# Windowed attention and a softplus feed-forward on one core: due times for the first 368 operations from a table, zero key columns by VectorE, the last block stored in smaller pieces

## The chip, the core and the metric

The kernel runs on one core of a Trainium2 chip. A core has five engines that work through queues of their own, in order: TensorE (PE in the profile; PEld is its weight load), VectorE (DVE), ScalarE (ACT), GpSimd (POOL) and SyncE (SP), which here only issues DMAs. ScalarE can issue DMAs too. The engines wait for each other and for DMAs by semaphores. The metric is the device time of one execution in microseconds (us).

## The reference

Attention with a causal window of 64 over 8 sequences of 576 positions, 8 heads of 64, and then a feed-forward layer with a softplus between its two products. All inputs and outputs are float32.

```python
scores = scale * np.matmul(q, k.transpose(0, 1, 3, 2))     # q, k, v: (8, 8, 576, 64)
mask = (rel >= 0) & (rel < window)                         # rel = query - key, window = 64
attn = softmax(np.where(mask, scores, -1e9))
x = np.matmul(attn, v)                                     # heads side by side: (4608, 512)
h = x @ w_in                                               # w_in: (512, 2048)
g = np.maximum(h, 0.0) + np.log1p(np.exp(-np.abs(h)))
out = g @ w_out                                            # w_out: (2048, 512)
```

## The kernel before

The 4608 rows are cut into 12 blocks `g` of 384 rows (three column tiles `j` of 128). The feed-forward's inner width is cut into 16 blocks `f` of 128. For every block of rows there are four head pairs `hp` of attention and then 16 steps of feed-forward. The first two blocks of rows work interleaved: block 0 with weight blocks 0 to 7, block 1 with all 16, block 0 with the rest (its partial sums wait in DRAM meanwhile), and then blocks 2 to 11 one after another.

All products are made in float32 accuracy from several passes: every operand is split into a rounded part and a remainder. The weights arrive as 64-bit words of 1 MB a block and are converted on the chip before they can be used.

The operations have these names, and the numbers behind them are the block and the head pair, or the block and the weight block:

- conversion of a weight block `f`: `load` (SP's DMA), `abs` (ScalarE, line 297), `c2`, `c3`, `c4` (VectorE, lines 298, 300, 302), `hi` (ScalarE, line 304), `lo` (VectorE, line 305)
- attention of a head pair: `q`, `k` (loads), `S` (PE, the scores, line 367 in the first three blocks, 411 later), `R` (VectorE, mask and row minima, line 338), `E` (ScalarE, exponentials, line 436), `sum` and `N` (VectorE, reciprocals and normalisation, lines 444 to 451), `T` and `cp` (in the first two blocks PE transposes, line 487, and ScalarE copies, line 490; later a DMA transposes), `V` (PE, the product with v, lines 498 and 590), `x0` and `x1` (the split of the result, ScalarE and VectorE, lines 504, 505)
- feed-forward step: `U` (PE, 12 matmuls of 384 columns, line 622), `soft` (ScalarE, three functions, lines 626 to 628), `m` (VectorE, line 634), `g0` (ScalarE in the first two blocks, line 636), `g1` (VectorE, line 637), `D` (PE, 9 matmuls of 512 columns into three banks, one for each `j`, line 646). `U` of a step writes one of two banks and waits until `m` of two steps before has read it.

No engine's queue is written by hand. Every operation is recorded with its engine, a planned cost, its dependencies and the buffers that it opens and uses, and a planner (`arrange`) lists them in time: of the operations that could start on an engine it takes the one with the earliest due time. The due times come from the function `dues` at first, and then eight rounds of `arrange` forward and `latest` backward follow, which give every operation the latest start that still meets the end. The round with the earliest planned end sets the order in which the instructions are issued. Constants of the planner are the delays `RESULT`, the DMA rate `BYTES_PER_US`, the delay `LAUNCH` and the first free time of each engine.

In the first block of rows there are no keys ahead of row 0. `load_k` lets GpSimd set the first 64 key columns to zero there (line 354), in four buffers, and loads the rest. GpSimd comes to it behind the masks and the zeros of `setup`.

The last step of a block copies the three banks of sums to SBUF (line 681) and stores them (line 684): tiles 0 and 1 in one DMA of 512 KB, tile 2 in one of 256 KB, both from SP.

Of the kernel before, what the change touches and what calls it, by code (L numbers as in the profile page):

```python
# [8 lines left out]
F32 = mybir.dt.float32  # L9
# [26 lines left out]

RESULT = {"PE": 0.25, "DVE": 0.12, "ACT": 0.15, "POOL": 0.2, "SP": 2.0}
BYTES_PER_US = 390e3
LAUNCH = 1.3

# [29 lines left out]
def arrange(ops, rings):  # L70

    for r in rings.values():
        r.taken = list(r.held)
    free = {"PE": 0.0, "DVE": 5.0, "ACT": 2.1, "POOL": 0.8, "SP": 0.8}
    pipe = 2.2
    left = {id(o): len(o.deps) for o in ops}
# [6 lines left out]
    while len(order) < len(ops):  # L83
        best = None
        for e, waiting in open_ops.items():
# [20 lines left out]
            t = max(free[e], min(at for at, _ in could))  # L106
            o = min((o for at, o in could if at <= t + 1e-9), key=lambda o: o.due)
            if best is None or t < best[0]:
# [7 lines left out]
        if o.nbytes:  # L116
            pipe = max(pipe, t + o.cost + LAUNCH) + o.nbytes / BYTES_PER_US
            o.end = pipe + RESULT["SP"]
        for b in o.opens:
# [55 lines left out]
def window_attention_softplus_ffn(  # L175
# [83 lines left out]
    def setup():  # L259
        nc.scalar.preload_act_table_set("natural_log_exp_and_others")  # L260
        nc.gpsimd.memset(wide, 0.0)
        for sign, op, base in ((1, ALU.is_gt, 0), (-1, ALU.is_ge, CH)):
            nc.gpsimd.affine_select(
                out=wide, in_=wide, pattern=[[sign, W]], compare_op=op, fill=FAR, base=base, channel_multiplier=-sign
            )
        nc.vector.memset(v_two[0][0:CH, 0, :], 0.0)
        for i in (1, 0, 2):
            nc.vector.tensor_copy(mask_q[0:CH, i, :], wide[0:CH, 0:P])
            nc.vector.tensor_copy(mask_q[CH:P, i, :], wide[CH:P, CH:W])
            if i:  # L270
                half = heads[i - 1]
                nc.vector.memset(mask_q[half, i, 0:CH], FAR)
# [12 lines left out]
    def convert(f):  # L285
# [28 lines left out]
    def attention(g, hp):  # L314
# [27 lines left out]
        if quad:  # L342
# [9 lines left out]
            def load_k():  # L352
                if skip:
                    nc.gpsimd.memset(qk(1)[:, 0:CH], 0.0)
# [26 lines left out]
        else:  # L381
# [22 lines left out]
            for j in range(NJ):  # L404
# [153 lines left out]
        for hh in range(2):  # L558
# [50 lines left out]
    sums_of, part, spilled = {}, {}, []  # L609
    ups, downs, stores = [], [], []  # L610

    def ffn(n, g, f, first, last):
# [12 lines left out]
        def soft():  # L625
# [24 lines left out]

        d = add("PE", 2.06, down, deps=[h, lo, *downs[-1:]], opens=acc if first else [], uses=[*gt, w_all[f]] + ([] if first else acc), name=f"D{g}.{f}")
# [141 lines left out]
```

## Time and profile before

| | us |
|---|---|
| median of 3 runs | 963.73 |
| lowest and highest of them | 963.46, 964.05 |
| the profiled execution | 965.21 |
| its span in the trace | 963.4 |
| mean granted clock of TensorE in it | 0.993 |

The profile shows one execution. Times are from the start of its span. A row of the timeline has the start, the length, the engine, the line and the operation with its tiles; where the engine was idle before it, the idle time and what ended it stand behind in brackets. Rows of equal instructions are merged (x24). Lines are those of the kernel before.

### The profile page before, as it was taken

How to read it: one execution, taken by the hardware profiler on the slowest of the kernel's cores; microseconds unless marked ns; L12 is line 12 of the kernel's file. 1: busy time of each engine (PE TensorE's matmuls, PEld its weight loads, DVE VectorE, ACT ScalarE, POOL GpSimd, SP SyncE). 2: the span in 40 equal slices, each digit the busy share in tenths (PEclk: the TensorE clock that was granted, in tenths of full speed). 3: DMA queues.
4: the chain of work that ended last, by engine and by line, in shares of the span. 5: the costliest groups of instructions: out<-in, count | busy, mean ns of one | idle time of the engine just before them, and what ended most of it. 6: DMA issues, size and time to landing. Idle time of an engine off the chain costs nothing.

```text
span 963.4 us, 16889 instructions
## 1 busy us (share of the span) xinstructions
PE 939.7 (98%) x6128; PEld 848.6 (88%) x6128; DVE 784.6 (81%) x1760; ACT 740.5 (77%) x1685; POOL 4.5 (0%) x18
## 2 busy tenths in 40 slices
PE   5899999999999999999999999999999999999997
PEld 4678888999999999998999999999999999998996
DVE  7999977898798888889879889879888887975333
ACT  6899877888788788778878778778878887875443
POOL 1000000000000000000000000000000000000000
PEclk7999999999999999999999999999999999999999
DMA  9961225575347345344445535535635464521000
GB/s 364 422 231 44 61 71 121 131 178 124 90 129 138 98 139 116 94 117 128 122 99 145 137 76 145 132 89 140 127 86 150 116 111 99 148 52 34 34 1 33
DMA packets 196516, 117.37 MB, mean 122 GB/s; under 512 B 130192, under 2 KB 187536, under 8 KB 194384
## 3 DMA queue, kind: packets, MB, share of 16 engines
q1 hardware_dynamic: 196144, 115.90, 46.0%
q8 instruction: 48, 0.79, 0.4%
q10 hardware_dynamic: 288, 0.39, 0.1%
q14 instruction: 36, 0.29, 0.1%
HBM read 74.58 MB, written 10.22 MB: 88 GB/s over the span
## 4 chain that ended last, share of the span: by engine, by line
PE 91%; DVE 6%; ACT 1%; issue 1%; POOL 0%; POOLq 0%; ACTq 0%
PE ps_o L646 40%; PE ps_h L622 40%; PE ps_a L590 6%; PE ps_a L411 5%; DVE work L300 1%; DVE work L302 1%; DVE w L305 1%; ACT st L436 1%; DVE st L338 1%; DVE work L298 1%; DVE u L634 0%; DVE g L637 0%; PE ps_a L367 0%; DVE st L451 0%; DVE x L505 0%
## 5 line engine op out<-in xcount | busy, mean ns | idle before, releaser
L622 PE MATMUL ps_h<-x,w 128*128 128x384 f32 x2304 | 435.2, 338 | 4.2 <-DVE u L634 3.2
L646 PE MATMUL ps_o<-w,g 128*128 128x512 f32 x1728 | 424.9, 394 | 0.0
L622 PEld LDWEIGHTS ps_h<-x,w 128*128 128x128 f32 x2304 | 401.9, 188 | 15.0 <-DVE u L634 3.9
L646 PEld LDWEIGHTS ps_o<-w,g 128*128 128x128 f32 x1728 | 320.3, 188 | 60.4 <-ACT u L626 0.2
L626 ACT ACTIVATE u<-ps_h 128x384 f32<-128x384 f32 x192 | 93.8, 488 | 138.2 <-PE ps_h L622 134.9
L634 DVE SCALAR_TENSOR_TENSOR u<-ps_h,u 128x384 f32<-128x384 f32 x192 | 106.3, 554 | 95.8 <-ACT u L628 93.5
L436 ACT ACTIVATE st<-st,mn 128x128 f32<-128x128 f32 x288 | 111.7, 389 | 24.2 <-DVE st L428 19.1
L637 DVE TENSOR_TENSOR g<-u,g 128x384 fp32r<-128x384 f32 x192 | 106.3, 554 | 10.1 <-ACT g L636 5.8
L628 ACT ACTIVATE u<-u 128x384 f32<-128x384 f32 x192 | 100.9, 525 | 6.1
L627 ACT ACTIVATE u<-u 128x384 f32<-128x384 f32 x192 | 100.8, 525 | 6.1
L338 DVE CUSTOM_DVE_ANT_0 st<-ps_a,wide 128x192 f32<-128x192 f32 x176 | 53.3, 351 | 13.8 <-PE ps_a L411 13.8
L636 ACT CAST g<-u 128x384 fp32r<-128x384 f32 x112 | 56.5, 505 | 9.8 <-DVE u L634 9.0
L590 PEld LDWEIGHTS <-v 128*128 128x128 bf16 x1136 | 54.5, 98 | 9.6 <-issue 7.2
L590 PE MATMUL ps_a<-tr,v 128*128 128x128 bf16 (+1 forms) x1136 | 60.3, 211 | 0.0
L411 PEld LDWEIGHTS ps_a<-k,q_hl 128*128 128x128 f32 x432 | 56.3, 191 | 2.4
L411 PE MATMUL ps_a<-k,q_hl 128*128 128x192 f32 x432 | 55.9, 271 | 0.0
L436 ACT ACTIVATION_READ_ACCUMULATOR st<-st,mn 128x1 f32 x288 | 53.9, 187 | 0.0
L451 DVE TENSOR_TENSOR st<-st,sm 128x768 f32<-128x768 f32 x48 | 45.9, 955 | 0.9
L549 DVE TENSOR_TENSOR v_in<-v_in,v 128x896 f32<-128x896 f32 x40 | 43.5, 1089 | 3.5 <-ACT v L548 3.1
L551 DVE TENSOR_TENSOR v<-v_in,v 64x896 bf16<-64x896 f32 x40 | 43.6, 1090 | 3.1 <-ACT v L550 1.6
L599 DVE TENSOR_TENSOR xf<-ps_a,xf 64x384 f32<-64x384 f32 x80 | 43.8, 548 | 1.5
L597 ACT COPY xf<-ps_a 64x384 f32<-64x384 f32 x80 | 38.1, 476 | 4.9 <-PE ps_a L590 3.1
(77 smaller groups left out, 754.2 us busy)
## 6 DMA issues: line engine op xcount, KB each, us to landing
v_in<-in_v_dram SPq DMA_DIRECT2D x80, 224.0 KB, 3.4
raw<-in_w_words_dram SPq DMA_DIRECT2D x16, 1024.0 KB, 13.9
k_in<-in_kT_dram SPq DMA_DIRECT2D x72, 224.0 KB, 3.6
q_in<-in_qT_dram SPq DMA_DIRECT2D x72, 192.0 KB, 3.4
out_dram<-raw SPq DMA_DIRECT2D x12, 512.0 KB, 4.0
out_dram<-raw SPq DMA_DIRECT2D x12, 256.0 KB, 4.0
v_two<-in_v_dram SPq DMA_DIRECT2D x3, 768.0 KB, 10.8
q_two<-in_qT_dram SPq DMA_DIRECT2D x8, 192.0 KB, 8.4
```

Source lines behind the costliest of these rows:

```text
L338: nc.vector.tensor_tensor_reduce(st()[:, hh, j, 0:width], scores, m, QSCALE, 3.0e38, ALU.add, ALU.min, mn()[:, hh, j : j + 1])
L411: mm(spv[:, hh, :], q_hl()[:, hh, j * P : (j + 1) * P], k_s[i]()[:, hh, j * P : j * P + W], start=(hh == 0 and i == 0), stop=(hh == 1 and ...
L436: nc.scalar.activation(sv()[:, i, 0:P], sv()[:, i, 0:P], AF.Exp, bias=mn()[:, hh, j : j + 1], scale=-1.0, accum_out=sm()[:, i : i + 1],)
L590: mm(av()[:, osl], (v3() if s else v12())[:, c, hh, :, :], src, start=(i == 0), stop=(i == len(passes) - 1), skip_group_check=True,)
L622: mm(hps()[:, :TB], weight(0, a, f)[:, c * P : (c + 1) * P], x[b][c](), start=(i_mm == 0), stop=(i_mm == 3 * NC - 1))
L626: nc.scalar.activation(u(), hps()[:, :TB], AF.Abs)
L627: nc.scalar.activation(u(), u(), AF.Exp, scale=-1.0)
L628: nc.scalar.activation(u(), u(), AF.Ln, bias=1.0)
L634: m = add("DVE", 0.47, lambda: stt(u(), hps()[:, :TB], 0.0, u(), ALU.max, ALU.add), deps=[s], uses=[hps, u], name=f"m{g}.{f}")
L636: lambda: (nc.scalar.copy if by_act else nc.vector.tensor_copy)(gt[0](), u()), deps=[m], opens=[gt[0]], uses=[u], name=f"g0.{g}.{f}")
L637: lo = add("DVE", 0.47, lambda: tt(gt[1](), u(), gt[0]().bitcast(F32), ALU.subtract), deps=[h], opens=[gt[1]], uses=[u, gt[0]], name=f"g1. ...
L646: mm(acc[j](), gt[a]()[:, j * P : (j + 1) * P], weight(1, b, f), start=(first and i == 0), stop=(last and i == 2),)
```

## The change

Three parts. First, the table `FIRST` holds due times for 368 operations, by their number in the order of recording: the conversions of all weight blocks (numbers 0 to 111, seven operations each, most of them), the attention of the first two blocks of rows and part of the third, and the first 97 feed-forward operations of the first steps. A ninth round takes these, and for the other operations the due times with which the best round so far was made. The planner's constants and some of its costs change as well (an SP result arrives 0.1 after a DMA's end instead of 2.0, the launch takes 2.8 instead of 1.3, loads cost 0.46 instead of 0.65), and ties go to the operation that was recorded first. Second, VectorE sets the zero columns in `setup`, and GpSimd no longer does in `load_k`. Third, `finish` replaces the copies and stores of the very last block: ScalarE copies tile 0 and VectorE tile 1, each stored by a DMA of 256 KB from SP; tile 2 is copied in halves, the first by VectorE and stored from SP, the second by ScalarE and stored from ScalarE's queue.

```diff
+FIRST = {
+    0: 19.59, 1: 35.33, 2: 11.55, 3: 0.86, 4: 18.33, 5: 37.88, 6: 9.86, 7: 27.81, 8: 35.83, 9: 45.39, 10: 28.25,
...
+}
-RESULT = {"PE": 0.25, "DVE": 0.12, "ACT": 0.15, "POOL": 0.2, "SP": 2.0}
-BYTES_PER_US = 390e3
-LAUNCH = 1.3
+RESULT = {"PE": 0.25, "DVE": 0.12, "ACT": 0.15, "POOL": 0.2, "SP": 0.1}
+BYTES_PER_US = 425e3
+LAUNCH = 2.8
...
-    free = {"PE": 0.0, "DVE": 5.0, "ACT": 2.1, "POOL": 0.8, "SP": 0.8}
-    pipe = 2.2
+    free = {"PE": 0.0, "DVE": 5.3, "ACT": 0.75, "POOL": 0.8, "SP": 0.75}
+    pipe = 0.0
...
-            pipe = max(pipe, t + o.cost + LAUNCH) + o.nbytes / BYTES_PER_US
-            o.end = pipe + RESULT["SP"]
+            o.end = pipe = max(pipe, t + LAUNCH) + o.nbytes / BYTES_PER_US
...
+        for _, k_slot in qk_slots:
+            nc.vector.memset(k_slot[:, 0:CH], 0.0)
         nc.vector.memset(v_two[0][0:CH, 0, :], 0.0)
...
             def load_k():
-                if skip:
-                    nc.gpsimd.memset(qk(1)[:, 0:CH], 0.0)
                 by.dma_start(qk(1)[:, skip:], kT[c0 : c0 + P, t0 - CH + skip : t0 + TB])
...
+    def finish(d, rows, acc):
+        o = [buf(ff, [P, 1, DM], w_words.dtype, "raw", n=2) for _ in range(2)]
+        half = DM // 2
+        for j in range(NJ):
+            for part_of, eng in (((0, DM), "ACT"),) if j == 0 else (((0, DM), "DVE"),) if j == 1 else (((0, half), "DVE"), ((half, DM), "ACT")):
+                to, queue = (nc.scalar, nc.scalar if j == 2 else nc.sync) if eng == "ACT" else (nc.vector, nc.sync)
+                a, b = part_of
...
+                c = add(eng, 0.6 if b - a == DM else 0.35, take, deps=[d], opens=[o[j // 2]] if j % 2 == 0 and a == 0 else [],
+                        uses=[acc[j]] + ([] if j % 2 == 0 and a == 0 else [o[j // 2]]), name=f"end{j}")
+                st = add("ACT" if queue is nc.scalar else "SP", 0.45,
+                         lambda queue=queue, view=view, j=j, a=a, b=b: queue.dma_start(rows[j * P : (j + 1) * P, a:b], view()),
+                         deps=[c], uses=[o[j // 2]], nbytes=(b - a) * P * 4, name=f"store{j}")
...
+        if n == len(steps) - 1:
+            finish(d, rows, acc)
+            return
...
-    for _ in range(ROUNDS):
+    for r in range(ROUNDS + bool(FIRST)):
+        if r == ROUNDS:
+            for i, o in enumerate(ops):
+                o.due = FIRST.get(i, best[2][i])
```

Three places show how the table and the rest move instructions. The first is VectorE's queue where it comes to weight block 0, among the softmax steps of the first block of rows. `sm` are the sums of a head pair's rows, `st` its scores, `work` a weight block in conversion (lines 298, 300, 302 are `c2`, `c3`, `c4`), `x1` the remainder of an attention result. Before, behind the minima of the fourth head pair:

```order
L444 TENSOR_SCALAR sm_228<-sm_228 128x6
L445 RECIPROCAL sm_228<-sm_228 128x6
L451 TENSOR_TENSOR st_81<-st_81,sm_228 128x768
L298 TENSOR_SCALAR work_265<-work_265 128x1024
L300 SCALAR_TENSOR_TENSOR work_265<-raw_134,work_265 128x1024
L302 SCALAR_TENSOR_TENSOR work_265<-raw_134,work_265 128x1024
L505 TENSOR_TENSOR x1_0_0_337<-ps_a_287,x0_0_0_323 128x384
```

The sums here are those of the third head pair (`sum0.2`, `N0.2`); weight block 0 follows them. With the change, behind the minima of the third head pair:

```order
L488 TENSOR_SCALAR sm_173<-sm_173 128x6
L489 RECIPROCAL sm_173<-sm_173 128x6
L495 TENSOR_TENSOR st_81<-st_81,sm_173 128x768
L344 TENSOR_SCALAR work_209<-work_209 128x1024
L346 SCALAR_TENSOR_TENSOR work_209<-raw_133,work_209 128x1024
L488 TENSOR_SCALAR sm_216<-sm_216 128x6
L489 RECIPROCAL sm_216<-sm_216 128x6
L495 TENSOR_TENSOR st_81<-st_81,sm_216 128x768
L348 SCALAR_TENSOR_TENSOR work_209<-raw_133,work_209 128x1024
```

The conversion of block 0 has moved ahead by two head pairs' sums: `c2.0` and `c3.0` stand behind `N0.0`, `c4.0` behind `N0.1`.

The second place is the beginning of ScalarE's queue, behind its two loads. Line 436 are the exponentials (x6 is a whole head pair), line 490 the copies `cp` of the transposed scores, line 297 is `abs`. Before:

```order
L436 ACTIVATE st_81,sm_175<-st_81,mn_154 128x128 x6
L436 ACTIVATE st_81,sm_204<-st_81,mn_196 128x128 x6
L436 ACTIVATE st_81,sm_228<-st_81,mn_208 128x128 x3
L490 COPY pt_239<-ps_a_224 128x384
L490 COPY pt_239<-ps_a_234 128x384
L436 ACTIVATE st_81,sm_228<-st_81,mn_208 128x128 x3
L297 ACTIVATE work_265<-raw_134 128x1024
```

And with the change (lines 480, 534, 343 and, for `hi`, 350):

```order
L480 ACTIVATE st_81,sm_173<-st_81,mn_164 128x128 x6
L343 ACTIVATE work_209<-raw_133 128x1024
L480 ACTIVATE st_81,sm_216<-st_81,mn_192 128x128 x6
L534 COPY pt_235<-ps_a_223 128x384
L480 ACTIVATE st_81,sm_238<-st_81,mn_205 128x128 x6
L534 COPY pt_235<-ps_a_231 128x384
L343 ACTIVATE work_272<-raw_203 128x1024
L350 CAST w_281<-work_209 128x1024
```

`abs0` stands ahead of the second head pair's exponentials instead of behind the third's, and `abs1` and `hi0` follow at once behind the third's.

The third place is the end of SP's queue, where a transpose and the stores of the last two blocks stand; behind each row are the semaphores that it waits for (DVE and Activation: the copies). Before:

```order
L523 DMA_TRANSPOSE tr<-nat 128x12x128 [waits DVE_49]
L684 DMA out_dram<-raw 128x512 [waits DVE_49]
L684 DMA out_dram<-raw 128x2x512 [waits Activation_49]
L684 DMA out_dram<-raw 128x512 [waits DVE_49]
L684 DMA out_dram<-raw 128x2x512 [waits Activation_49]
```

The last two rows are the last block's. And with the change:

```order
L752 DMA out_dram<-raw 128x512 [waits DVE_49]
L752 DMA out_dram<-raw 128x2x512 [waits Activation_49]
L673 DMA out_dram<-raw 128x512 [waits DVE_49]
L673 DMA out_dram<-raw 128x512 [waits DMAHW0_49,Activation_49]
L673 DMA out_dram<-raw 128x256 [waits DMAHW2_49,DVE_49]
```

Before, the small store (tile 2) stood ahead of the large one. Now tile 1's stands first, then tile 0's, then the first half of tile 2's; the second half's is the last row of ScalarE's queue. In ScalarE's queue the copy of that half waits for VectorE's copy of the first half.

More of the change, by code (lines that the diff above doesn't have):

```diff
@@ L73, in arrange @@
         r.taken = list(r.held)
-    free = {"PE": 0.0, "DVE": 5.0, "ACT": 2.1, "POOL": 0.8, "SP": 0.8}
-    pipe = 2.2
+    for i, o in enumerate(ops):
+        o.at = i
+    free = {"PE": 0.0, "DVE": 5.3, "ACT": 0.75, "POOL": 0.8, "SP": 0.75}
+    pipe = 0.0
     left = {id(o): len(o.deps) for o in ops}
@@ L106, in arrange @@
             t = max(free[e], min(at for at, _ in could))
-            o = min((o for at, o in could if at <= t + 1e-9), key=lambda o: o.due)
+            o = min((o for at, o in could if at <= t + 1e-9), key=lambda o: (o.due, o.at))
             if best is None or t < best[0]:
@@ L293, in bits @@
             return work().bitcast(U32)
-        a = add("SP", 0.45, lambda: nc.sync.dma_start(raw(), w_words[f]), opens=[raw], nbytes=1024 * 1024, name=f"load{f}")
+        a = add("SP", 0.5, lambda: nc.sync.dma_start(raw(), w_words[f]), opens=[raw], nbytes=1024 * 1024, name=f"load{f}")
         a.ahead = True
@@ L352, in load_k @@
             def load_k():
-                if skip:
-                    nc.gpsimd.memset(qk(1)[:, 0:CH], 0.0)
                 by.dma_start(qk(1)[:, skip:], kT[c0 : c0 + P, t0 - CH + skip : t0 + TB])
-            lq = add("SP", 0.65, lambda: nc.sync.dma_start(qk(0), qT[c0 : c0 + P, rows_t]), deps=waits, opens=[slot],
+            lq = add("SP", 0.46, lambda: nc.sync.dma_start(qk(0), qT[c0 : c0 + P, rows_t]), deps=waits, opens=[slot],
                      uses=[two["q_in"], two["k_in"], *far], nbytes=192 * 1024, name=f"q{tag}")
-            lk = add("ACT" if by is nc.scalar else "SP", 0.65, load_k, deps=waits, opens=[],
+            lk = add("ACT" if by is nc.scalar else "SP", 0.46, load_k, deps=waits, opens=[],
                      uses=[slot, two["k_in"], *far], nbytes=224 * 1024, name=f"k{tag}")
@@ L418, in minima @@
                         scaled_min(hh, j, sp()[:, hh * W : (hh + 1) * W])
-                before = add("PE", 0.45, scores, deps=[qh, ql, kh, kl, before], opens=[sp] if j else [sp, st, mn], uses=[q_hl, *k_s], name=f"S{tag}")
+                before = add("PE", 0.44, scores, deps=[qh, ql, kh, kl, before], opens=[sp] if j else [sp, st, mn], uses=[q_hl, *k_s], name=f"S{tag}")
                 rdeps.append(add("DVE", 0.56, minima, deps=[before],
@@ L595, in attention @@
             ds = heads[hh]
-            p = add("PE", 0.7, products, deps=[t0_, t1_, c1, c2, c3, c4, c5, p], opens=[av] if hh else [av, xf], uses=[tr, v12, v3], name=f"V{tag}")
+            p = add("PE", 0.675, products, deps=[t0_, t1_, c1, c2, c3, c4, c5, p], opens=[av] if hh else [av, xf], uses=[tr, v12, v3], name=f"V{tag}")
             y = add("ACT", 0.5, lambda ds=ds, av=av: nc.scalar.copy(xf()[ds, :], av()[D:P, :TB]), deps=[p],
@@ L610, in window_attention_softplus_ffn, with view, take @@
     ups, downs, stores = [], [], []
+    def finish(d, rows, acc):
[5 more added lines that the diff above has]
+                a, b = part_of
+                def view(j=j, a=a, b=b):
+                    return o[j // 2]().bitcast(F32).rearrange("p m (j n) -> p (m j) n", n=DM)[:, j % 2, a:b]
+                def take(to=to, view=view, j=j, a=a, b=b):
+                    (to.copy if to is nc.scalar else to.tensor_copy)(view(), acc[j]()[:, a:b])
+                c = add(eng, 0.6 if b - a == DM else 0.35, take, deps=[d], opens=[o[j // 2]] if j % 2 == 0 and a == 0 else [],
[3 more added lines that the diff above has]
+                         deps=[c], uses=[o[j // 2]], nbytes=(b - a) * P * 4, name=f"store{j}")
+                stores.append((len(steps) - 1, st))
     def ffn(n, g, f, first, last):
@@ L630, in ffn @@
         by_act = g < 2 or f % 2
-        a = add("PE", 2.09, up, deps=[o for hp in range(NP) for o in x_ops[g, hp]] + converted[f] + ups[-1:], opens=[hps],
+        a = add("PE", 2.1, up, deps=[o for hp in range(NP) for o in x_ops[g, hp]] + converted[f] + ups[-1:], opens=[hps],
                 uses=[b for i in range(2) for b in x[i]] + [w_all[f]], name=f"U{g}.{f}")
@@ L649, in down @@
                     )
-        d = add("PE", 2.06, down, deps=[h, lo, *downs[-1:]], opens=acc if first else [], uses=[*gt, w_all[f]] + ([] if first else acc), name=f"D{g}.{f}")
+        d = add("PE", 2.075, down, deps=[h, lo, *downs[-1:]], opens=acc if first else [], uses=[*gt, w_all[f]] + ([] if first else acc), name=f"D{g}.{f}")
         ups.append(a)
@@ L734, in window_attention_softplus_ffn @@
     dues(times)
-    for _ in range(ROUNDS):
-        for (p, n), r in rings.items():
-            r.held = [b for key, b in two.items() if b.ring is r]
+    for r in range(ROUNDS + bool(FIRST)):
+        if r == ROUNDS:
+            for i, o in enumerate(ops):
+                o.due = FIRST.get(i, best[2][i])
+        for ring in rings.values():
+            ring.held = [b for b in two.values() if b.ring is ring]
         order = arrange(ops, rings)
@@ L740, in window_attention_softplus_ffn @@
         if best is None or end < best[0]:
-            best = (end, [(o, o.start) for o in order])
+            best = (end, order, [o.due for o in ops])
         latest(order, end)
@@ L746, in window_attention_softplus_ffn @@
         setup()
-        for o, at in best[1]:
+        for o in best[1]:
             o.fn()
```

40 rows, old and new, of the table FIRST are left out of this document.

## The prediction

> **What bounds the kernel now.** I read the page's busy times first, then busy time by stretch, then PE's waits in the first 100 us, then the timeline around them.
>
> ```profile
> span 963.4 us, 16889 instructions
> PE 939.7 (98%) x6128; PEld 848.6 (88%) x6128; DVE 784.6 (81%) x1760; ACT 740.5 (77%) x1685; POOL 4.5 (0%) x18
> ```
>
> PE idles 963.4 - 939.7 = 23.7 us in all. The stretches (length, then busy us of PE, PEld, DVE, ACT, POOL, the granted clock, the DMA share, GB/s) tell where.
>
> ```profile
> 10.00:20.00 10.00, 5.63 (x68) 4.49 (x69) 8.82 (x32) 9.10 (x40) 0.00 (x0) 0.61 1.04 408
> 20.00:30.00 10.00, 8.55 (x116) 7.03 (x113) 8.60 (x12) 7.54 (x12) 0.00 (x0) 0.88 1.02 415
> 60.00:80.00 20.00, 18.29 (x170) 14.78 (x169) 19.83 (x51) 18.27 (x49) 0.00 (x0) 1.00 0.14 33
> 400.00:800.00 400.00, 400.00 (x2508) 364.79 (x2508) 342.86 (x773) 317.11 (x718) 0.00 (x0) 1.00 0.49 117
> ```
>
> In the middle PE is busy without a break, and its work there is the same in both kernels. From 30 to about 100 us PE still has holes and VectorE has none (19.83 of 20): VectorE converts the weight blocks, and PE takes what it delivers. Before 30 us VectorE idles too, 1.18 + 1.40 = 2.58 us between 10 and 30. So only three things can move the time: where the start's queues put PE when it becomes dense, small costs between PE's blocks in the dense part, and the tail behind the last matmul.
>
> ```profile
> PE ps_a L367 <- POOL k_two L354: 5.2, 1, 5.2
> ```
>
> **The first scores.** This row of PE's waits says that its first matmul waits for GpSimd's zero columns. Timeline rows (start, length) and the first key load, from issue to landing:
>
> ```profile
> 0.90 0.48 DVE L266 MEMSET v_two<- 64x512 f32 x1 [0.90 <-PEq L779]
> 5.07 0.11 DVE L272 MEMSET mask_q<- 64x64 bf16 x1
> 5.00 0.23 POOL L354 MEMSET k_two<- 128x64 f32 x2
> 5.21 1.56 PE L367 MATMUL ps_a<-k_two,q_two 64*64 64x128 f32 x24 [5.21 <-POOL k_two L354]
> 6.82 0.29 DVE L338 CUSTOM_DVE_ANT_0 st<-ps_a,mask_q 128x128 f32<-128x128 f32 x1 [1.64 <-PE ps_a L367]
> k_two<-in_kT_dram ACTq DMA_DIRECT2D x2, 192.0 KB, 3.8
> ```
>
> The load is issued at 0.77 and lands 3.8 later, at 4.6. With the zeros gone from GpSimd, PE starts then, 0.6 earlier, and VectorE's first minima come at 6.2 instead of 6.82. The four memsets now stand on VectorE ahead of its masks. VectorE's memset of 64x64 takes 0.11 and that of 64x512 0.48; four of 128x64 cost between 0.4 and 1.9, and I take 0.5, near the small one. The masks end with the row at 5.07, at 5.2, so 0.5 is hidden behind the load and PE's first 1.56; at 1.9 the start would gain nothing (+0.6).
>
> **The early order.** Before, VectorE did all its softmax work of the first three head pairs before it touched a weight block. In the new order the first block's `c2`, `c3` and `c4` stand between softmax steps, where VectorE idled, and ScalarE's multiply `abs0` stands ahead of the second head pair's exponentials. If this fills the 2.58 us apart from some 0.3 of short gaps behind dependent instructions, VectorE is 0.6 + 2.3 = 2.9 us ahead of its old self at equal work done. That is the most; nothing is gained if ScalarE's results come late (a slip of 2.9).
>
> What PE gets of it depends on the op that it waits for last. VectorE's pitches, start to start, are read here:
>
> ```profile
> 65.30 1.22 DVE L305 TENSOR_TENSOR w<-work,w 128x1024 fp32r<-128x1024 f32 x1
> ...
> 68.03 0.16 DVE L444 TENSOR_SCALAR sm<-sm 128x6 f32<-128x6 f32 x1
> ...
> 69.33 0.28 DVE L338 CUSTOM_DVE_ANT_0 st<-ps_a,mask_q 128x128 f32<-128x128 f32 x1
> ...
> 70.60 1.22 DVE L305 TENSOR_TENSOR w<-work,w 128x1024 fp32r<-128x1024 f32 x1
> 71.73 0.55 DVE L505 TENSOR_TENSOR x<-ps_a,x 128x384 fp32r<-128x384 f32 x1
> 72.20 0.55 DVE L637 TENSOR_TENSOR g<-u,g 128x384 fp32r<-128x384 f32 x1
> 72.67 0.69 DVE L298 TENSOR_SCALAR work<-work 128x1024 uint32<-128x1024 uint32 x1
> 73.27 0.55 DVE L634 SCALAR_TENSOR_TENSOR u<-ps_h,u 128x384 f32<-128x384 f32 x1
> 73.74 1.21 DVE L300 SCALAR_TENSOR_TENSOR work<-raw,work 128x1024 uint32<-128x1024 uint32 x1
> ```
>
> `lo` takes 1.13, `g1` and `m` 0.47 each, `c2` 0.60, the sums with the normalisation 1.30 (68.03 to 69.33); `c3` and `c4` are as long as `lo` and get its 1.13. The row at 65.30 is `lo6`, which releases `U0.6`. In the new queue one more of each of `sum`, `N`, `c2`, `c3`, `c4`, `lo`, `m`, `g1` stands ahead of it: 1.30 + 0.60 + 3 x 1.13 + 2 x 0.47 = 6.2. So `lo6` comes at 65.3 + 6.2 - 2.9 = 68.6 and `U0.6` 1.3 later, at 69.9. From there to `U1.4` PE has 6 `U`, 2 `D`, one `V` and one `S`.
>
> ```profile
> 73.81 0.92 PE L498 MATMUL ps_a<-pt,v_two 128*64 128x64 f32 x24
> ...
> 89.49 0.89 PE L367 MATMUL ps_a<-k_two,q_two 64*64 64x128 f32 x24
> 91.21 2.35 PE L622 MATMUL ps_h<-x,w 128*128 128x384 f32 x12 [0.83 <-DVE u L634]
> ```
>
> With `U` 2.11 and `D` 2.09 (next fence: 2.12, 2.07) that is 12.7 + 4.2 + 0.9 + 0.9 = 18.7. `D0.6` waits some 0.25 for its `g1`, so `U1.4` starts at 88.8. In the old run it is the last op that waits, at 91.21; there `S2.1` (0.89) is already done, in the new order not. So PE is 91.2 - 88.8 - 0.9 = 1.5 us ahead when it becomes dense, of VectorE's 2.9; the rest goes to VectorE work that was moved forward. ScalarE is nearly as full (18.27 of 20), and where I walk the new queues by these pitches, its result comes only 0.1 to 0.4 before VectorE needs it at several ops. I take a slip of 0.5: **-1.0**, with ends -1.8 (nothing slips, the first load lands a little sooner) and +1.4 (all 2.9 lost).
>
> **Between PE's blocks.** The planner's constants changed too, so all later blocks are reordered. A stretch of the dense part:
>
> ```profile
> 375.09 2.28 PE L622 MATMUL ps_h<-x,w 128*128 128x384 f32 x12
> 377.21 2.23 PE L646 MATMUL ps_o<-w,g 128*128 128x512 f32 x9
> 379.28 1.52 PE L590 MATMUL ps_a<-tr,v 128*128 128x64 bf16 x28
> 380.64 2.36 PE L622 MATMUL ps_h<-x,w 128*128 128x384 f32 x12
> 382.84 2.26 PE L646 MATMUL ps_o<-w,g 128*128 128x512 f32 x9
> ```
>
> Start to start, a `U` takes 2.12 behind a `D` and 2.20 behind the bf16 products `V`: 0.08 for leaving a `V`. Counted in the two orders, `V` is followed by `U` or `D` 44 times before and 33 now, -0.9; 21 times it is now followed by scores, a pair that the old order doesn't have, 0 to 0.08 each, 0 to +1.7. Scores are left 61 times before, 65 now, nothing to speak of. I take **-0.3**, near the shown rows, with -0.9 and +0.8 as ends.
>
> **The tail.** The last `D` ends column block by column block.
>
> ```profile
> 957.64 0.59 ACT L681 COPY raw<-ps_o 128x512 f32<-128x512 f32 x1 [2.76 <-PE ps_o L646]
> 958.34 0.69 DVE L681 COPY raw<-ps_o 128x512 f32<-128x512 f32 x1 [0.69 <-PE ps_o L646]
> 959.06 0.81 SPq L684 DMA_DIRECT2D out_dram<-raw  x2
> ```
>
> Both stores start at 959.06, though the last copy for the 512 KB one, ScalarE's, ended at 958.23: it stands behind the 256 KB one in SP's queue. DMA then runs at full share until 962.0, and the span ends 1.4 later.
>
> ```profile
> 961.00:962.00 1.00, 0.00 (x0) 0.00 (x0) 0.00 (x0) 0.00 (x0) 0.00 (x0) 0.52 0.98 371
> ```
>
> Now the middle block's store stands first and goes at 958.4, when its VectorE copy ends, the first block's right behind. The data is the same 768 KB at that row's 371 GB/s, so it ends about 0.7 sooner if it flows without a hole. The last half's ScalarE copy waits for VectorE's half (its semaphore in the order): 958.34 + 0.35 (half of 0.69) + 0.1 + 0.4 (over half of 0.59) = 959.2, 0.1 later than the old last copy, but only 128 KB hang on it. **-0.7**, with ends -1.0 and 0.
>
> [...]
>
> **Sum.** -1.0 - 0.3 - 0.7 = -2.0. The profiled execution took 965.21 (span 963.4), so its like would take 963.2; the median of the runs, 963.73, lies 1.48 lower, so 961.7.
>
> **Rivals.** *The lead is lost:* the new order puts conversions ahead of exponentials on ScalarE, and if sums, `hi` casts and loads come late, VectorE idles as before while it has more work ahead of `lo6`: +1.4 - 0.3 - 0.7 = +0.4, 964.1. For it speaks ScalarE's 9.10 of 10 between 10 and 20 us; against it that VectorE has other work first at most of these places. *Everything fits:* -1.5 - 0.9 - 0.8 = -3.2, 960.5. *Slower:* the new dense order lets PE run dry. Its price is a wait of about 0.7 in each of the ten blocks from the third on, 961.7 + 7 = 968.7; it decides once a `V` or `S` stands ahead of the VectorE or transpose result that it needs. Against it, VectorE is 86% busy there (342.86 of 400) and the old order never waited. *The clock:* it was 0.61 and 0.88 of full between 10 and 30 us, and it came back here, while PE, busy from 18.34 on, had hardly a gap:
>
> ```profile
> 18.34 1.55 PE L498 MATMUL ps_a<-pt,v_two 128*64 128x64 f32 x24 [1.91 <-ACT st L436]
> 22.00:23.00 1.00, 0.90 (x5) 0.43 (x4) 0.30 (x2) 0.91 (x3) 0.00 (x0) 0.82 0.97 407
> ```
>
> In the new order PE pauses for copies between all of `V0.0` to `V0.3`, so it may stay low to about 30: two scores at 1.56 instead of 0.89 and most of `U0.0` at half speed, +3, of which `U0.2`'s wait for `m0.0` hides about 1.9: 962.8.
>
> [...]
>
> **How the numbers follow.** Forecast 961.7 (960.7 to 962.7): 0.48. Everything fits, 960.5: 0.15. Lead lost, 964.1: 0.20. Low clock, 962.8: 0.08. PE runs dry, 968.7: 0.09. The range 960.0 to 964.4 leaves out the last and some of the second. A measurement tells 0.2% from no change: 961.8 and 965.7 are the bounds. Faster takes three fifths of the forecast, the second case and a little of the others, 0.47; slower is PE running dry, 0.09; same is 0.44.
>
> **What would show it.** PE's first matmul near 4.6 and VectorE's near 6.2; VectorE busy over 9.5 of 10 between 10 and 30 us; `lo6` near 69, `U1.4` near 89; PE 400 of 400 between 400 and 800; stores issued from 958.4 less the lead, and about 4.4 from the last matmul to the end instead of 5.1. VectorE idle before 30 us would make the first term wrong, a PE wait behind 100 us the second, a last store that lands 2 us after its issue the third.

## The result and the profile after

The changed kernel took 970.09 us (median of 6 runs, 969.26 to 971.68), the kernel before 963.81 beside it (6 runs). The ratio is 1.0065 with an interval of 1.0052 to 1.0078: 6.3 us slower, where 961.7 was forecast and 964.4 was the end of the range. The profiled execution took 970.17, its span 5.0 more than that of before; the trace of before is of an execution of 965.21 us, 1.4 above the 963.81, and that is the rest of the 6.3. Lines in the rows of the changed kernel are its own: `S` is L411 and L455, `T` L531, `V` L542 and L634, `U` L687, `D` L711, `m` L699, `g1` L702, `lo` L351.

The first page, and busy time by stretch (length; PE, PEld, DVE, ACT, POOL; granted clock, DMA share, GB/s):

```profile
span 968.4 us, 16905 instructions
PE 942.4 (97%) x6128; PEld 848.9 (88%) x6128; DVE 788.6 (81%) x1764; ACT 744.0 (77%) x1686; POOL 4.1 (0%) x14
```

```profile
10.00:20.00 10.00, 4.92 (x53) 3.87 (x55) 9.76 (x26) 9.04 (x36) 0.00 (x0) 1.00 1.04 397
20.00:30.00 10.00, 7.29 (x120) 6.11 (x117) 8.23 (x11) 7.09 (x17) 0.00 (x0) 1.00 1.02 422
60.00:80.00 20.00, 17.77 (x171) 14.92 (x169) 19.83 (x33) 17.07 (x34) 0.00 (x0) 1.00 0.05 17
100.00:190.00 90.00, 87.59 (x623) 76.47 (x622) 70.86 (x149) 71.36 (x148) 0.00 (x0) 1.00 0.40 96
400.00:800.00 400.00, 399.63 (x2522) 362.69 (x2522) 344.15 (x775) 320.52 (x727) 0.00 (x0) 1.00 0.50 119
```

PE idles 26.0 us where it idled 23.7, and is counted busy 2.7 longer for the same matmuls: the 5.0 are about half idle time and half longer busy time. The row from 100 to 190 is new; before, PE had no break there:

```profile
100.00:190.00 90.00, 90.00 (x621) 79.89 (x620) 73.85 (x143) 72.65 (x159) 0.00 (x0) 1.00 0.40 94
```

**Where it went.** For a table by place I take PE's start of an operation less a fixed duration for each operation that PE issued before it (`U` 2.09, `D` 2.065, the others by their shortest pitch). This is what PE had lost until then, whatever the order; the table has its difference to before. All differences are to the one trace of before, whose execution lies 0.8 to 1.4 us above the medians of before that the experiments had beside them; against the median run of before a kernel's loss is that much larger than its row. e7's own trace is 1.9 above its median. The kernels of the experiments below are in the table too.

| kernel | U1.4, 91 us | U1.10, 122 us | U2.0, 190 us | U11.15, last |
|---|---|---|---|---|
| changed | +0.3 | +2.7 | +3.8 | +5.6 |
| old order (e1) | -0.1 | -0.1 | -0.1 | -0.1 |
| new to U1.4, then old (e2) | +0.9 | +0.9 | +0.8 | +0.8 |
| old to U1.4, then new (e3) | -0.5 | +1.8 | +2.4 | +4.1 |
| old to U2.0, then new (e8) | -0.6 | -0.2 | -0.2 | +1.5 |
| no table (e4) | +0.3 | +2.8 | +4.4 | +6.2 |
| new DMA model only (e5) | +0.5 | +2.4 | +2.2 | +6.5 |
| old DMA model, no table (e6) | -0.4 | -0.4 | -0.6 | -1.1 |
| 1 us of margin, no table (e7) | +1.4 | +2.1 | +1.9 | +0.5 |
| 2 us of margin, no table (e12) | +0.3 | +1.3 | +1.5 | -0.3 |
| e6 to U2.0, then e7 (e9) | -0.1 | -0.1 | -0.3 | -1.6 |

So the changed kernel lost little at the start, 2.4 between 91 and 122 us, about 1.4 between 173 and 190 (not a column; 0.3 came back in between), and 1.8 in the blocks from `U2.0` on; the new tail gave 0.6 back.

**The waits between 91 and 190 us.** Timeline rows around PE's two waits at 106 and 109, SyncE's queue ahead of them, and the rows around the wait at 181:

```profile
91.41 0.64 SPq L584 DMA_DIRECT2D v_in<-in_v_dram  x1
92.83 0.33 SPq L752 DMA_DIRECT2D part<-raw  x1
93.62 1.66 SPq L567 DMA_TRANSPOSE tr<-nat  x1
95.33 0.62 SPq L584 DMA_DIRECT2D v_in<-in_v_dram  x1
```

```profile
100.94 0.94 ACT L592 CAST v<-v_in 128x896 bf16<-128x896 f32 x1 [3.33 <-DMA v_in<-in_v_dram]
101.91 1.09 DVE L593 TENSOR_TENSOR v_in<-v_in,v 128x896 f32<-128x896 f32 x1 [1.47 <-ACT v L592]
105.90 1.89 PE L711 MATMUL ps_o<-w,g 128*128 128x512 f32 x7 [0.72 <-DVE g L702]
109.06 1.14 PE L687 MATMUL ps_h<-x,w 128*128 128x384 f32 x5 [0.57 <-DVE u L699]
...
171.70 0.83 ACT L571 CAST nat<-st 128x768 bf16<-128x768 f32 x1 [1.67 <-DMA tr<-nat]
172.56 0.96 DVE L572 TENSOR_TENSOR st<-st,nat 128x768 f32<-128x768 f32 x1 [1.95 <-ACT nat L571]
180.67 1.66 PE L687 MATMUL ps_h<-x,w 128*128 128x384 f32 x8 [1.00 <-DVE u L699]
```

Read from the bottom of each group: PE waits for VectorE, VectorE had waited for ScalarE, and ScalarE for a DMA. The second half of `v2.0` was issued at 95.33, behind a store and a transpose, and landed at 100.84; ScalarE's cast of it stood at the head of its queue from 97.6 on, with a conversion's cast and a `g0` behind it. At 171.70 it is a transpose that lands late. Before, ScalarE waited for no DMA behind 60 us; here it does so eight times, 11.8 us in all, and PE's waits behind 100 us come to 2.5. That the late landings cause PE's waits is read from this one trace here; the experiments on single loads below test it.

**The planner's landings.** The planner puts a load of 224 KB at 0.65 + 1.3 + 0.59 + 2.0 = 4.54 us after its issue with the constants of before, and at 2.8 + 0.54 = 3.34 with the new ones. For all of SyncE's DMAs issued behind 60 us, the time from issue to landing in the trace, less the same time in the planner's result:

| | loads of q, k, v | longer than planned | mean | transposes | longer than planned | mean |
|---|---|---|---|---|---|---|
| before | 226 | 17 | -0.97 us | 80 | 2 | -1.87 us |
| changed | 228 | 177 | +0.37 us (up to 2.17) | 80 | 40 | +0.08 us (up to 2.32) |

The new constants are nearer to the mean, and so half of the transposes and most of the loads now take longer than the planner allows for. They come late for an operation that the planner put right behind them; most of them hold nobody up, as ScalarE's eight waits show.

### The profile page after: what moved, and what is told of

It is laid out like the page before. It is cut to its first block, busy times and chain, and to the rows that moved or that the text cites. A ratio compares the mean times of both kernels' runs of the same rounds, so it can differ in the third digit from the quotient of the medians.

```text
span 968.4 us, 16905 instructions
## 1 busy us (share of the span) xinstructions
PE 942.4 (97%) x6128; PEld 848.9 (88%) x6128; DVE 788.6 (81%) x1764; ACT 744.0 (77%) x1686; POOL 4.1 (0%) x14
## 4 chain that ended last, share of the span: by engine, by line
PE 83%; DMA 7%; DVE 6%; ACT 2%; issue 1%; SPq 1%; DVEq 0%; ACTq 0%
PE ps_h L687 37%; PE ps_o L711 36%; PE ps_a L634 5%; PE ps_a L455 5%; DMA raw<-in_w_words_dram 4%; DMA q_two<-in_qT_dram 1%; DMA v_in<-in_v_dram 1%; DMA v_two<-in_v_dram 1%; DVE u L699 1%; DVE work L348 1%; DVE st L384 1%; DVE g L702 1%; DVE work L346 0%; DMA k_in<-in_kT_dram 0%; DVE v L595 0%
## 5 line engine op out<-in xcount | busy, mean ns | idle before, releaser
L687 PE MATMUL ps_h<-x,w 128*128 128x384 f32 x2304 | 432.6, 338 | 3.1 <-DVE u L699 2.1
L711 PE MATMUL ps_o<-w,g 128*128 128x512 f32 x1728 | 427.8, 394 | 0.8 <-DVE g L702 0.7
L687 PEld LDWEIGHTS ps_h<-x,w 128*128 128x128 f32 x2304 | 402.8, 188 | 15.1 <-DVE u L699 5.1
L711 PEld LDWEIGHTS ps_o<-w,g 128*128 128x128 f32 x1728 | 318.7, 188 | 62.7 <-DVE g L702 2.7
L699 DVE SCALAR_TENSOR_TENSOR u<-ps_h,u 128x384 f32<-128x384 f32 x192 | 106.5, 555 | 98.7 <-ACT u L693 97.3
L702 DVE TENSOR_TENSOR g<-u,g 128x384 fp32r<-128x384 f32 x192 | 106.6, 556 | 17.7 <-ACT g L701 12.7
L634 PEld LDWEIGHTS <-v 128*128 128x128 bf16 x1136 | 54.9, 98 | 10.7 <-issue 9.6
L634 PE MATMUL ps_a<-tr,v 128*128 128x128 bf16 (+1 forms) x1136 | 62.1, 211 | 0.0
L455 PEld LDWEIGHTS ps_a<-k,q_hl 128*128 128x128 f32 x432 | 56.3, 191 | 2.6
L455 PE MATMUL ps_a<-k,q_hl 128*128 128x192 f32 x432 | 58.6, 274 | 0.0
```

The costliest lines, as they stand in the source:

```text
L455: mm(spv[:, hh, :], q_hl()[:, hh, j * P : (j + 1) * P], k_s[i]()[:, hh, j * P : j * P + W], start=(hh == 0 and i == 0), stop=(hh == 1 and ...
L634: mm(av()[:, osl], (v3() if s else v12())[:, c, hh, :, :], src, start=(i == 0), stop=(i == len(passes) - 1), skip_group_check=True,)
L687: mm(hps()[:, :TB], weight(0, a, f)[:, c * P : (c + 1) * P], x[b][c](), start=(i_mm == 0), stop=(i_mm == 3 * NC - 1))
L699: m = add("DVE", 0.47, lambda: stt(u(), hps()[:, :TB], 0.0, u(), ALU.max, ALU.add), deps=[s], uses=[hps, u], name=f"m{g}.{f}")
L702: lo = add("DVE", 0.47, lambda: tt(gt[1](), u(), gt[0]().bitcast(F32), ALU.subtract), deps=[h], opens=[gt[1]], uses=[u, gt[0]], name=f"g1. ...
L711: mm(acc[j](), gt[a]()[:, j * P : (j + 1) * P], weight(1, b, f), start=(first and i == 0), stop=(last and i == 2),)
```

## The experiments

All kernels have the changed kernel's zero columns and tail. Ratios are to the kernel before on the same chip; 0.001 is 0.96 us.

### Whose order: the first 91 us or the rest

In e1, e2, e3 and e8 the planner is replaced by a list of all 3067 operations, taken from the two planners' results, in e2 and e3 the one's first part and then what is left in the other's order:

```diff
-    for r in range(ROUNDS + bool(FIRST)):
...
+    order = [ops[i] for i in LIST]
     with tc.manual_schedule():
         setup()
-        for o in best[1]:
+        for o in order:
             o.fn()
```

> The order of before on every engine, written out as a list, with the changed kernel's zero columns by VectorE and its new tail. All theories: the tail gives 0.55 (4.55 from the last matmul to the end where it was 5.1), the zero columns 0 to 0.6, so 962.6 to 963.3 beside 963.8. If the loss came from the zero columns or the tail and not from an order, it stays at 968 or more.

> The changed kernel's order up to U1.4 (91 us), then what is left in the order of before. Theory 'later order' (the new order behind 91 us costs the 5.2 us that PE loses there): PE stands 0.4 behind at U1.4 and loses nothing more, 963.8 + 0.4 - 0.55 = 963.7. Rival 'early order' (the first 91 us leave VectorE with work undone, and PE pays for it later under any order): 968 or more.

> The order of before up to U1.4, then what is left in the changed kernel's order. Theory 'later order': the 5.2 us come back, 962.9 + 5.2 = 968.1. Rival 'early order': about as the old order throughout, 963.

Measured: e1 0.9993 (0.9984 to 1.0002), e2 1.0017 (1.0008 to 1.0025), e3 1.0043 (1.0030 to 1.0056). In us against before: -0.7, +1.6, +4.1. "Later order" holds: with the old order behind `U1.4` PE loses nothing more (e2's row of the table stays at 0.8 to the end), with the new one it loses 4.6 (e3). The early order costs more than I expected of it, 0.9 at `U1.4` instead of 0.4, and in e2's trace the new tail gains nothing (5.1 us from the last matmul to the end, where e1 has 4.5). Kernels with the same early order differ by some 0.5 there (e1, e3, e8: -0.1, -0.5, -0.6; changed, e2: +0.3, +0.9), which is how well one trace tells it.

The fourth empties the table (`FIRST = {}`), so that the best of the planner's eight rounds under the new constants stands:

> The changed kernel with an empty table: the planner's own best round under the new constants sets the order from the start. If the table's numbers cost the time, 964 or less; if the planner's new constants (and the order behind the first 368 operations that they give) cost it, 968 to 970, within 1.5 of the changed kernel.

Measured: 971.29 us, ratio 1.0078 (1.0064 to 1.0091). So it is the constants and not the table. The table itself gains 0.6 in the traces and 1.2 by the ratios, whose intervals overlap; by the planner's own sum it gained 4.0 (963.49 to 959.52).

The last of this group changes over only at `U2.0`:

> The order of before up to U2.0 (190 us), then the changed kernel's. Theory 'exits': from U2.0 on only the new sequence of PE's blocks costs, V left for U, D or S 44 times instead of 36 and small waits, 1.8 in all, so 1.1 to 1.3 above the 964.4 of before (the tail's 0.6 off). Rival 'the waits before 190 us are all': as the old order throughout, 963.8 to 964.1.

Measured: 1.0015 (1.0006 to 1.0024), +1.4 us, a little over the 1.1 to 1.3; PE loses 1.7 behind `U2.0`, as "exits" said. These rows of the changed kernel's timeline show one:

```profile
377.87 1.03 PE L455 MATMUL ps_a<-k,q_hl 128*128 128x192 f32 x8
378.74 2.27 PE L687 MATMUL ps_h<-x,w 128*128 128x384 f32 x12
380.85 1.52 PE L634 MATMUL ps_a<-tr,v 128*128 128x64 bf16 x28
382.21 0.67 PE L455 MATMUL ps_a<-k,q_hl 128*128 128x192 f32 x4
382.72 2.27 PE L711 MATMUL ps_o<-w,g 128*128 128x512 f32 x9
```

Two scores behind a `D` take 0.87 start to start (377.87 to 378.74), 0.435 each; one behind `V` takes 0.51 (382.21 to 382.72). Over all blocks from `U2.0` on, what follows a `V` takes 0.085 (`S`), 0.099 (`D`) or 0.108 us (`U`) more than its shortest pitch. `V` is left 36 times in the old order and 44 times in the new one, 3.62 and 4.32 us, so 0.7 of the 1.8. The rest is small: `U` and `D` behind `U` or `D` come 1.1 later in sum, of which 0.4 are waits.

### Which constants: the planner's DMA model

```diff
-RESULT = {"PE": 0.25, "DVE": 0.12, "ACT": 0.15, "POOL": 0.2, "SP": 0.1}
-BYTES_PER_US = 425e3
-LAUNCH = 2.8
+RESULT = {"PE": 0.25, "DVE": 0.12, "ACT": 0.15, "POOL": 0.2, "SP": 2.0}
+BYTES_PER_US = 390e3
+LAUNCH = 1.3
...
-            o.end = pipe = max(pipe, t + LAUNCH) + o.nbytes / BYTES_PER_US
+            pipe = max(pipe, t + o.cost + LAUNCH) + o.nbytes / BYTES_PER_US
+            o.end = pipe + RESULT["SP"]
```

This is e6, with the table empty. e5 is the reverse in the kernel before: only these lines as in the changed kernel, nothing else of the planner. e7 and e12 keep the new constants, empty the table and plan each landing later:

```diff
-            o.end = pipe = max(pipe, t + LAUNCH) + o.nbytes / BYTES_PER_US
+            pipe = max(pipe, t + LAUNCH) + o.nbytes / BYTES_PER_US
+            o.end = pipe + 1.0
```

> The kernel before with the new zero columns and tail, and of the planner only the new DMA model (result 0.1 instead of 2.0, launch 2.8 for 1.3, 425 for 390 GB/s, the issue no longer counted). Against the two traces, the planner of before puts a v load's landing at 4.54 us after its issue where it takes 3.43, and a transpose's at 5.76 where it takes 3.85; with the new model it plans 3.34 and 3.73 where they take 3.68 and 3.73. Theory 'no margin' (consumers queued for a landing that comes late stop their engine): 968 to 972 beside 964.4. Rival 'other constants' (the costs of operations, start times, tie-break): 963.5 to 965.

> The changed kernel with an empty table and the planner's DMA model of before; all its other new constants stay. Theory 'no margin': 963 to 965.5 beside 964.4, where the empty table with the new model gave 971.3; ScalarE no longer waits for loads behind 60 us. Rival 'other constants': 968 to 971.

> The changed kernel with an empty table and the new DMA model, but every landing planned 1.0 us later. Theory 'no margin': most of the 7 us beyond before go, 963.5 to 966.5. Rival 'chance of the planner' (each set of constants gives another order, good or bad, whatever the margin): no tie to the margin, 968 or more is as likely.

> As the run with 1.0 us of margin, with 2.0. Theory 'no margin': landings are about 1 us later than planned at most places, so a second us brings little: 962.5 to 965. Rival 'chance of the planner': no tie to the margin, 960 to 972.

| | us | ratio | interval |
|---|---|---|---|
| e5, new DMA model only | 971.10 | 1.0072 | 1.0060 to 1.0085 |
| e6, old DMA model, other constants new | 963.86 | 0.9994 | 0.9985 to 1.0003 |
| e7, new model, 1.0 us of margin | 963.25 | 0.9991 | 0.9982 to 1.0000 |
| e12, new model, 2.0 us of margin | 964.78 | 1.0006 | 0.9997 to 1.0015 |

The times of "no margin" come out (e7 ends 0.25 below its range; and the landings that e12's text puts 1 us late are 0.4 late in the mean, by the table above), and "other constants" falls: these few lines alone make the kernel before as slow as the changed one, and undoing them or adding 1 us to every landing takes all of it away. That any change to the planner would have cost as much falls with it: three different orders with a margin lie within 1 us of before. In e5 the cost stands at other places than in the changed kernel. PE's rows that wait for a transpose:

```profile
456.19 0.47 PE L589 MATMUL ps_a<-tr,v 128*128 128x128 bf16 x6 [0.82 <-DMA tr<-nat]
521.40 1.17 PE L589 MATMUL ps_a<-tr,v 128*128 128x64 bf16 x21 [1.52 <-DMA tr<-nat]
```

These two are 2.3 of the 6.0 us that e5 loses behind `U1.4`. Another 1.9 goes between `U1.4` and `U1.10`, where PE, ScalarE and VectorE wait for no DMA at all. So the runs show that these lines cost the time; that it is lost through landings that come late is shown for a part only. The rest comes with the other order that the planner makes when it expects its loads sooner, and by which step of it stays open.

The exits follow the model too: counted from `U2.0` on, `V` is left 36 times under the old model (before and e6), 38 and 36 times with margin (e7, e12), 44 in the changed kernel and 56 in e5. Why an early landing makes the planner break up pairs of `V` I did not look into. The exits aren't what the margin gains, though: e7 leaves `V` 38 times and is still 1.3 ahead of before from `U2.0` on. e12's +0.6 comes from the stretch ahead of `U2.0` (+1.5 there) and from a tail of 5.0 us; in between this order loses the least of those in the table.

### One late load, and one early one

e10 keeps the changed kernel's order but for SyncE's two loads of `v2.0`:

```diff
-SP: ... store0, v2.0, store0, tr0.2.0, v2.0, tr1.2.0 ...
+SP: ... v2.0, v2.0, store0, store0, tr0.2.0, tr1.2.0 ...
```

> The changed kernel's order with one edit: on the DMA queue's engine both v2.0 loads stand ahead of the stores of the first half's sums, instead of one between them and one behind a transpose. In the changed kernel the second landed at 100.9, ScalarE waited 3.33 us for it, and PE then waited 0.72 and 0.57 for VectorE. Theory 'late landing': these waits go, U1.10 comes 2.2 earlier (122.3), and 967.9 beside 970.1. Rival 'VectorE's order' (PE waits whatever lands when): 969.5 to 970.1.

Measured: 968.90 us, 1.0047 (1.0034 to 1.0060). ScalarE's wait of 3.33 and PE's of 0.72 are gone; of the two PE waits this is left:

```profile
108.08 3.22 PE L799 MATMUL ps_h<-x,w 128*128 128x384 f32 x17 [0.44 <-DVE u L811]
```

`U1.7` comes 0.98 sooner although the start of this execution was 0.55 later, so the landing cost 1.5 of the 2.3 between `U1.4` and `U1.7`. Of the rest, 0.44 is the wait in this row, for an `m` that VectorE reaches late; "late landing" was right in kind and two thirds in size.

The same loss comes without a late load, however. In e3 this cast of `v2.0` runs at 87.13 and ScalarE waits for no DMA between 60 and 125 us, yet PE waits at the same two places and loses 2.2 between `U1.4` and `U1.7`:

```profile
105.08 1.87 PE L823 MATMUL ps_o<-w,g 128*128 128x512 f32 x7 [0.72 <-DVE g L814]
108.24 4.43 PE L799 MATMUL ps_h<-x,w 128*128 128x384 f32 x24 [0.59 <-DVE u L811]
```

There VectorE works without a pause from 96.89 to 107.64 and comes late to the `g1` and the `m` all the same. e4 loses 2.5 between `U1.4` and `U1.10`, and none of its engines but SyncE waits for a DMA there. So a late load is one way to this loss, and a fuller VectorE queue at that place is another.

For the wait at 181 the kernels do agree. Where the changed kernel has ScalarE waiting 1.67 for the transpose and PE waiting 1.00, e3, e4 and e10 have 1.11 and 0.46, 1.87 and 1.19, 1.75 and 1.09: PE's wait is ScalarE's less 0.65 to 0.68 each time.

e11 asks the same of the start. In the changed kernel `V0.0` waits 1.97 us for its v, whose last two loads stand behind the second weight block's. The list sets all three v loads together ahead of it, so the first of them, which stood behind `load0`, moves back:

```diff
-SP: ... load0, v0.0, k1.0, q0.3, k0.3, k1.3, load1, v0.0, v0.0, load5 ...
+SP: ... load0, k1.0, q0.3, k0.3, k1.3, v0.0, v0.0, v0.0, load1, load5 ...
```

> The changed kernel's order up to U1.4 and then the order of before, with one edit: the last two of the first v loads stand ahead of the second weight block's load, not behind it. Theory 'late v load': V0.0's wait of 1.97 goes, V0.0 at 17.0 to 17.2, PE's pauses before U0.0 shrink and U1.4 comes about 1 us earlier than 92.1: 965.0 beside 964.4 of before, 1.0 below the same order without the edit. Rival 'amount of work' (VectorE has more ahead of U1.4 in this order, and no landing matters): 966.0, as without the edit.

Measured: 967.53 us, 1.0033 (1.0021 to 1.0046), 1.5 worse than e2. The wait is gone and `V0.0` starts at 17.23, 2.4 us sooner than in e2; yet `U0.0` comes at 35.66 instead of 34.78 and `U1.4` is 1.0 later. So this late load isn't what cost the start its lead. In its place PE now works at half clock from 24 to 34 us:

```profile
24.00:34.00 10.00, 8.07 (x100) 6.64 (x96) 9.86 (x14) 8.11 (x18) 0.00 (x0) 0.50 1.02 419
```

Whether the clock, or the later `load1`, made it worse is open.

### A version that beats both

e9 is the old DMA model's order (e6) up to `U2.0` and then what is left in the order with 1.0 us of margin (e7); e13 the same with e12's.

> The order of the empty table with the old DMA model up to U2.0 (there 0.62 us ahead of before), then what is left in the order with 1.0 us of margin (from U2.0 on it lost 1.32 us less than before). If the stretches add as they did until now: 0.62 + 1.32 + 0.55 (tail) = 2.5 below before, 961.9 beside 964.4. Rival: what is left undone at U2.0 differs in the two orders and costs the second gain, 963.2.

> The order of the empty table with the old DMA model up to U2.0, then what is left in the order with 2.0 us of margin, which from U2.0 on lost 0.46 us less than the one with 1.0. If the stretches add: 0.46 below the first combination, 1.6 + 0.46 = 2.1 below before. Rival (work left over at U2.0 differs and costs it): level with the first combination, 1.6 below, or less.

> The first combination once more, unchanged: ratio 0.998 to before, 1.6 us below it, if the gain is the order's; within 0.1% of before if it was that call's.

Measured: e9 0.9981 (0.9972 to 0.9990) and again 0.9982 (0.9973 to 0.9991), e13 0.9981 (0.9972 to 0.9990): 962.75, 962.50 and 962.48 us, 1.7 to 1.8 below before. The gain repeats. In the traces the stretches nearly add: the first trace of e9 has 0.3 of e6's 0.6 at `U2.0`, all of the later 1.3 and the tail, a span of 961.2 where before has 963.4. The medians are only 1.6 apart, because the traced execution of before lies 0.85 above the median of its runs here and e9's 0.26. e13's further 0.5 did not come (from `U2.0` on it gains 1.4, e9 1.3). PE's row of before is back in e9, busy 90.00 of the 90 us:

```profile
100.00:190.00 90.00, 90.00 (x589) 79.84 (x588) 74.20 (x141) 72.35 (x150) 0.00 (x0) 1.00 0.41 98
```

## Why the prediction was wrong, point by point

**The first scores: right, and worth less than thought.** Timeline rows of the changed kernel:

```profile
4.20 1.56 PE L411 MATMUL ps_a<-k_two,q_two 64*64 64x128 f32 x24 [4.20 <-DMA k_two<-in_kT_dram]
...
5.80 0.29 DVE L384 CUSTOM_DVE_ANT_0 st<-ps_a,mask_q 128x128 f32<-128x128 f32 x1 [0.89 <-PE ps_a L411]
```

PE starts at 4.20 (forecast 4.6), VectorE at 5.80 (6.2), and the load is waited for now. With the old order (e1, e3, e8) this 1.0 us has shrunk to 0.1 to 0.6 at `U1.4`: in e1 PE's third score waits 1.89 for the next load.

**The early order: -1.0 forecast, about +0.3 measured at `U1.4`, by the first rival.** The step that failed here is the filling of VectorE's idle time. VectorE idles 0.24 + 1.77 = 2.01 us between 10 and 30, not 0.3: most of it is one stop of 1.64 at 23.80 for ScalarE's exponentials, which stand behind a `cp` that waited for PE. `lo6` then starts at 70.30 where 68.6 was worked out, 1.7 later, and the idle time that wasn't filled is as long:

```profile
23.80 0.17 DVE L488 TENSOR_SCALAR sm<-sm 128x6 f32<-128x6 f32 x1 [1.64 <-ACT st L480]
...
70.30 1.22 DVE L351 TENSOR_TENSOR w<-work,w 128x1024 fp32r<-128x1024 f32 x1
...
70.19 0.60 PE L687 MATMUL ps_h<-x,w 128*128 128x384 f32 x2
71.57 2.00 PE L687 MATMUL ps_h<-x,w 128*128 128x384 f32 x10 [0.78 <-DVE w L351]
...
84.37 0.96 PE L687 MATMUL ps_h<-x,w 128*128 128x384 f32 x4 [0.31 <-DVE u L699]
```

`U0.6` starts at 70.19 (forecast 69.9), but only with two matmuls that don't read what `lo6` writes; the other ten wait for it. (In the old run too it starts 0.95 behind `lo6`, not 1.3.) The step behind it, from `lo6` to `U1.4`, was nearly right: 20.4 us where 20.2 was worked out, with one more wait of 0.31.

**Between PE's blocks: -0.3 forecast, +5.3 measured.** This is the step that failed and put the time out of the range. I treated the new constants as a reordering whose only price is the change from one block of matmuls to the next. For that alone the price was right (0.08 for leaving `V`; 0.085 to 0.108 measured), but I put scores behind `V` near nothing, and they cost 0.085. Of the changed kernel's 1.8 from `U2.0` on, this accounts for 0.7. The larger part, 3.5 between 91 and 190 us, I had not looked for. Late landings make some 2.5 of it (1.5 by e10, 1.0 in the wait at 180.67), and the rest isn't traced to one step. "In the middle PE is busy without a break, and its work there is the same in both kernels" is true of before, and I carried it over to an order that the same planner made with less time for its loads. A row that would have warned of the landings was there. The page of before lists the loads (count, size, median us to landing):

```profile
v_in<-in_v_dram SPq DMA_DIRECT2D x80, 224.0 KB, 3.4
```

The new constants plan 3.34 for this, a little less than the median, so at least about half had to come late; the old ones planned 4.54.

**The rivals.** "PE runs dry" had the right sign and, with 968.7, nearly the time, but by the wrong place and cause, so the closeness is luck: I priced a wait of 0.7 in each of ten dense blocks and spoke against it with VectorE's 86%. The waits are few (0.72, 0.57 and 1.00 us behind 100 us are the three longest), they lie where the weights are still converted, and each stands behind a late DMA in this trace, though e3 has the first two without one. "The clock" came true in part: the granted clock is 0.51 from 33 to 36.5 us, during `U0.0`.

**The tail: right but for 0.1.** From the last matmul to the end 4.5 us instead of 5.1 (forecast 4.4):

```profile
962.51 0.59 ACT L668 COPY raw<-ps_o 128x512 f32<-128x512 f32 x1 [2.07 <-PE ps_o L711]
963.20 1.11 DVE L668 COPY raw<-ps_o 128x512 f32<-128x512 f32 x2 [2.16 <-PE ps_o L711]
963.91 1.30 SPq L673 DMA_DIRECT2D out_dram<-raw  x3
964.34 0.37 ACT L668 COPY raw<-ps_o 128x256 f32<-128x256 f32 x1 [1.25 <-DVE raw L668]
964.75 0.38 ACTq L673 DMA_DIRECT2D out_dram<-raw  x1
```

The first store goes when VectorE's copy of the middle block ends, as worked out, and ScalarE's half copy waited 1.25 for VectorE's. The store that lands last is not the one behind that copy but SyncE's third, issued at 964.83 behind the other two and landed 2.55 later, 0.26 after ScalarE's. With the old order (e1) the gain is the same; in the traces of e2, e6, e11 and e12 the tail is 5.1, 4.9, 5.2 and 5.0 us, and why most of the gain is missing there is open.

## What to carry to other kernels

When a planner fixes the order of queues that are served in order, its duration for a DMA is not an estimate but a promise: what is planned for the mean landing is late about half the time (40 of 80 transposes here), and where the engine has already come to it, it stops all that stands behind (ScalarE's queue for 3.33 us at `v2.0`). Here 1 us more in the plan for each landing was worth 8 us, and constants nearer to the mean cost 7. Only a part of this can be laid to single late landings (2.5 of 5.3 us in the changed kernel); the rest is the order that such a plan leads to, and how is open. Whoever predicts a change to such constants should first compare the planned landings with the trace's, DMA by DMA, and ask what stands behind each consumer; the planner's own end time was no guide here: it gave the table 4.0 us for at most about 1, and it put e5's end at 961.0 and e12's at 964.0, where e5 ran 6 us longer than e12.

## What the hardware showed that was not expected

The granted clock of the changed kernel reads 1.00 from the start, although three transposes at 16 us take 0.87 where they take 0.49 at 70 us, and 24 scores 1.56 at 4.20 where they take 0.89 at 29.39. The first entry for the clock in its trace stands at 22.79 and sets it to full; the 1.00 that this profile shows ahead of it does not fit these durations. The clock was halved at 33.03 and was full again by 37. Windows of the changed kernel (length; PE, PEld, DVE, ACT, POOL; clock, DMA share, GB/s):

```profile
16.00:17.00 1.00, 0.87 (x3) 0.50 (x3) 0.93 (x3) 1.00 (x2) 0.00 (x0) 1.00 1.18 354
30.00:31.00 1.00, 0.52 (x14) 0.22 (x5) 1.00 (x3) 1.00 (x3) 0.00 (x0) 1.00 1.05 442
31.00:32.00 1.00, 0.18 (x2) 0.00 (x0) 1.00 (x4) 0.78 (x2) 0.00 (x0) 1.00 0.97 410
32.00:33.00 1.00, 0.39 (x15) 0.42 (x18) 1.00 (x8) 1.00 (x2) 0.00 (x0) 1.00 1.00 426
33.00:34.00 1.00, 1.00 (x19) 0.67 (x11) 1.00 (x3) 1.00 (x7) 0.00 (x0) 0.52 0.97 387
```

```profile
16.11 0.87 PE L531 MATMUL ps_o<-ident,st 128*128 128x128 f32 x3 [1.93 <-DVE sm L488]
...
29.39 0.89 PE L411 MATMUL ps_a<-qk_far 64*64 64x128 f32 x24 [0.78 <-DMA qk_far<-in_qT_dram]
...
69.95 0.49 PE L531 MATMUL ps_a<-ident,st 128*128 128x128 f32 x3
```

PE was busy for 1.09 of the 3.00 us from 30 to 33, and its longest pause between 20 and 33 was 1.43. What halved the clock is not shown by these rows.
